# Attention and two mixtures of experts: maxima across partitions by TensorE, filler matmuls in blocks, two banks for batch 0's values, batch 1 held back

## The chip, the cores and the metric

The kernel runs on one core of a Trainium2 chip. Its time is the device time of one execution in microseconds, and of several executions the median counts. Five engines share the work: TensorE (PE in the profile; PEld are its weight loads), VectorE (DVE), ScalarE (ACT), GpSimd (POOL) and SyncE (SP, which here only issues DMAs). Each takes its instructions in the order in which they were written for it, and an instruction that waits holds up all behind it on its engine.

## The reference, cut to what matters

Three stages follow each other:

```python
# attention: 4 batches, 8 heads, 576 tokens, head size 64, float32
scores = q @ k.T / 8                       # heads 0-3: the last 32 keys; heads 4-7: every 32nd key
attn = softmax(where(mask, scores, -1e9))
x = (attn @ v)                             # written as 2304 tokens x 512
# first mixture: all 4 experts on all tokens
x = sum_e p[:, e:e+1] * (relu(x @ w1[e]) @ w2[e])      # 512 -> 1024 -> 512
# second mixture: 8 experts, each token goes to one (288 tokens each, by sorted gate logits)
out[mask_e] = relu(x[mask_e] @ v1[e]) @ v2[e]
```

Matrices of the mixtures are held as two float16 halves (a high part and what is left over), and a product takes three float16 matmuls. To make the halves, a tensor is first scaled by a power of two, which is found from its largest absolute value: a maximum along each partition, then one across the 128 partitions.

## The kernel before, in words

A small planner (class `Stream`) writes the program. Each task is a Python generator; it issues instructions, and yields how long it expects to wait. The planner keeps a clock of its own (`st.now`), advanced by the expected cost of every matmul, and `run`, `pick` and `till` keep a queue time for each other engine. So the order of instructions on every engine is fixed when the program is built, by the planner's costs. Nothing of the planner runs on the chip, where only the order and the data dependences count.

Attention works in units of two heads (`hp` 0 to 3: units 0 and 1 are local heads, 2 and 3 strided ones), in two halves each. A unit's q and k are turned by TensorE (`turn`, tiles `pk`, `pq`); for batch 0 this takes nine instructions for a turn, for later batches three. A half (`half_unit`) then computes scores (`pss`, 12 matmul instructions), masks and takes the row maximum on VectorE (L401), exponentiates on ScalarE (L407), multiplies by the reciprocal sums (L420; `pick` chooses VectorE or GpSimd), turns the probabilities (`turn_p`, tile `pp`), multiplies by the values (`po`), and splits the result into `xh` and `xl` (L452, L453). Batch 0's tiles of `po` use one PSUM bank.

While attention of batch 0 runs, weights of the first expert are loaded, their maximum is found (`measure`, `widest`), and they are split into `wh` and `wl` (`split`). The main loop starts layer 1 of expert 0 when batch 0's attention and this split are written. From then on TensorE does expert matmuls (`pl` of layer 1, `py` of layer 2), and the attention of batches 1 to 3 is written between them. Tokens of an expert go in five groups (512, 512, 256, 512, 512), and group 1 of expert 0 needs batch 1.

`widest` (L217) finds a maximum across partitions by GpSimd's `partition_all_reduce` (L224), and VectorE then computes the scale (L230 to L236). `load_gate` (L713) scales the gate's weights in this way. `keep_warm` (L466) is called when the planner has a gap, and writes matmuls that nobody reads; with the gaps that the planner sees, the program has none of them. A loop of the planner starts at L976.

## Time and profile before

| what | value |
|---|---|
| median of 3 runs | 1216.44 us (1211.65 to 1218.27) |
| profiled execution, its own time | 1209.59 us |
| its span, first to last instruction | 1207.9 us |
| PE busy | 1159.6 us, 96% |
| DVE busy | 767.3 us, 64% |
| ACT, POOL busy | 525.0 us (43%), 221.3 us (18%) |
| mean granted TensorE clock | 0.976 |

The span is cut by the profile into 40 slices, and busy shares are given for each. PEclk is the share of TensorE's full clock that was granted: 1.0 is 2.4 GHz, 0.5 is 1.2 GHz. Ends of matmuls are modelled and overlap, so the start of one to the start of the next is a better measure of what one costs than its duration. A bracket behind an instruction tells how long its engine was idle before it and whom it waited for; "issue" is idle time that no wait shown explains.

### The profile page before, as it was taken

The numbers are of one execution on the slowest core, as the hardware profiler recorded it, in microseconds if no ns is written. First come the engines' busy times: TensorE is split into PE (matmuls) and PEld (weight loads), VectorE is DVE, ScalarE is ACT, GpSimd is POOL, SyncE is SP. The second block draws the span as 40 slices with busy tenths as digits, with TensorE's granted clock in tenths as the row PEclk, the third lists the DMA queues.
The fourth block names the chain that finished last, engine by engine and source line by source line (L and its number), as shares of the span: only waits on it lengthen the run. The fifth ranks groups of instructions, "written<-read, shape, count | busy, mean of one in ns | idle before, by whom it ended". The sixth has DMA issues, their size and how long they took to land.

```text
span 1207.9 us, 20992 instructions
## 1 busy us (share of the span) xinstructions
PE 1159.6 (96%) x7989; PEld 684.8 (57%) x7989; DVE 767.3 (64%) x2186; ACT 525.0 (43%) x1151; POOL 221.3 (18%) x346
## 2 busy tenths in 40 slices
PE   8939999999999999999999999999989899999998
PEld 6726565664444464444464445654534477777887
DVE  3849986737675557675568877874367766666310
ACT  3637555523542424453444356645323333333444
POOL 3021300010101111111110001010034332334333
PEclk9858999999999999999999999999999999999999
DMA  9342454211338434444732242321003354555631
GB/s 234 76 118 61 100 186 83 77 50 62 113 105 278 140 140 139 140 139 167 252 122 88 71 139 84 126 97 62 1 36 112 119 176 164 180 180 179 248 111 41
DMA packets 87774, 150.84 MB, mean 125 GB/s; under 512 B 48313, under 2 KB 53689, under 8 KB 85626
## 3 DMA queue, kind: packets, MB, share of 16 engines
q1 hardware_dynamic: 74106, 104.09, 28.1%
q0 software_dynamic: 13568, 45.41, 10.5%
q8 instruction: 63, 1.03, 0.4%
q14 instruction: 37, 0.30, 0.1%
HBM read 106.44 MB, written 45.37 MB: 126 GB/s over the span
## 4 chain that ended last, share of the span: by engine, by line
PE 78%; DVE 6%; issue 2%; POOL 1%; DMA 1%; ACT 0%; POOLq 0%; ACTq 0%
PE py L123 35%; PE pl L123 34%; PE pss L123 1%; DVE ohr L1307 1%; PE po L123 1%; PE pp L127 1%; PE pc L123 1%; PE pyt L127 1%; PE pxt L127 1%; DMA out_dram<-ot,ix 1%; DVE ge L1150 1%; PE pi L123 1%; PE th L123 0%; PE pcs L123 0%; PE po L127 0%
## 5 line engine op out<-in xcount | busy, mean ns | idle before, releaser
L123 PE MATMUL py<-wh,h 128*128 128x512 f16 x1024 | 311.5, 379 | 0.9 <-DVE h L639 0.9
L123 PEld LDWEIGHTS <-h 128*128 128x128 f16 x1600 | 148.6, 98 | 168.0 <-DVE h L639 1.4
L123 PE MATMUL pl<-xh,wh 128*128 128x512 f16 (+1 forms) x640 | 229.5, 359 | 0.0
L123 PE MATMUL pl<-xl,wh 128*128 128x512 f16 (+1 forms) x640 | 229.3, 358 | 0.0
L123 PE MATMUL pl<-xh,wl 128*128 128x512 f16 (+1 forms) x640 | 229.3, 358 | 0.0
L123 PE MATMUL py<-wl,h 128*128 128x512 f16 x512 | 194.1, 379 | 0.0
L123 PEld LDWEIGHTS <-wh 128*128 128x128 f16 x1280 | 124.2, 98 | 117.3 <-issue 0.3
L635 ACT ACTIVATE t<-pl 128x512 f32<-128x512 f32 (+1 forms) x160 | 88.8, 555 | 213.7 <-PE pl L123 203.9
L639 DVE TENSOR_TENSOR h<-t,h 128x512 f16<-128x512 f32 (+1 forms) x144 | 91.4, 639 | 87.0 <-ACT h L636 87.0
L123 PE MATMUL pl<-xT,wa 128*128 128x288 f16 x768 | 108.3, 289 | 0.0
L123 PE MATMUL py<-hT,wb 128*128 128x288 f16 (+2 forms) x864 | 106.6, 273 | 0.2 <-POOL hT L1414 0.2
L925 ACT ACTIVATE po<-pr,v_s 128x1024 f16<-128x1024 f32 x64 | 73.1, 1150 | 70.2 <-DVE v_s L236 30.6
L123 PEld LDWEIGHTS <-wl 128*128 128x128 f16 x640 | 62.5, 98 | 58.4 <-issue 0.4
L927 DVE SCALAR_TENSOR_TENSOR po<-pr,v_s,po 128x1024 f16<-128x1024 f32 x64 | 82.0, 1282 | 18.4 <-ACT po L925 18.2
L123 PEld LDWEIGHTS <-wb 128*128 128x128 f16 x864 | 73.4, 98 | 14.5 <-issue 0.5
L123 PEld LDWEIGHTS <-wa 128*128 128x128 f16 x768 | 71.5, 99 | 17.4 <-issue 0.3
L636 ACT ACTIVATE h<-pl 128x512 f16<-128x512 f32 (+1 forms) x144 | 78.7, 547 | 0.0
L912 DVE TENSOR_REDUCE pam<-pr 128x1 f32<-128x1024 f32 x64 | 76.5, 1208 | 0.0
L407 ACT ACTIVATE sm<-sm,mx 96x128 f32<-96x128 f32 (+2 forms) x152 | 58.0, 388 | 19.4 <-DVE mx L401 19.4
L677 DVE SCALAR_TENSOR_TENSOR ysb<-py,pe,ysb 128x512 f32<-128x512 f32 x42 | 31.5, 749 | 46.2 <-PE py L123 45.9
L1414 POOL TENSOR_TENSOR hT<-t,hT 128x288 f16<-128x288 f32 x64 | 49.1, 780 | 35.4 <-ACT hT L1413 26.3
L1412 ACT ACTIVATE t<-pl 128x288 f32<-128x288 f32 x64 | 26.2, 409 | 61.9 <-PE pl L123 55.9
(293 smaller groups left out, 1572.0 us busy)
## 6 DMA issues: line engine op xcount, KB each, us to landing
pr<-in_moe_w_dram SPq DMA_DIRECT2D x64, 512.0 KB, 4.0
raw<-in_moe_w_dram SPq DMA_DIRECT2D x32, 512.0 KB, 7.6
w1d<-po POOLq DMA_DIRECT2D x32, 512.0 KB, 5.2
w2d<-po POOLq DMA_DIRECT2D x32, 512.0 KB, 5.1
wa<-w1d SPq DMA_DIRECT2D x8, 2048.0 KB, 8.2
wb<-w2d SPq DMA_DIRECT2D x8, 2048.0 KB
yd<-yr SPq DMA_DIRECT2D x18, 257.0 KB, 6.3
qn<-in_q_dram SPq DMA_DIRECT2D x24, 144.0 KB, 2.9
```

The source lines that it names most:

```text
L123: nc.tensor.matmul(o, a, b, start=first, stop=last)
L127: nc.tensor.transpose(o, a, i)
L407: nc.scalar.activation(sm[j][0:nq, t, 0:nk], sm[j][0:nq, t, 0:nk], AF.Exp, bias=mx[0:nq, 0, j, t:t + 1], scale=-1.0, accum_out=mx[0:nq, 1, ...
L635: nc.scalar.activation(t[:, 0:n], pl[:, 0:n], AF.Relu, scale=HS)
L636: nc.scalar.activation(hh[:, 0, 0:n], pl[:, 0:n], AF.Relu, scale=HS)
L639: nc.vector.tensor_sub(hh[:, 1, 0:n], t[:, 0:n], hh[:, 0, 0:n])
L677: nc.vector.scalar_tensor_tensor(ysb[:, j], py, pe, ysb[:, j], op0=ALU.mult, op1=ALU.add)
L912: nc.vector.tensor_reduce(am[:, c:c + 1], chunks[4 * m + c], AX.XY, ALU.max, apply_absolute_value=True)
L925: nc.scalar.activation(h, r, AF.Copy, scale=s_)
L927: nc.vector.scalar_tensor_tensor(l, r, s_, h, op0=ALU.mult, op1=ALU.subtract)
L1412: nc.scalar.activation(t, pl, AF.Relu, scale=HS)
L1414: nc.gpsimd.tensor_sub(hT[:, f, 1], t, hT[:, f, 0])
```

## The change

Six things change in the program's text.

1. `widest` no longer calls GpSimd. TensorE transposes the 128 per-partition maxima (spread over 128 columns) into a PSUM tile `pm`, and VectorE reduces it. All 30 uses take this path.
2. Fillers: `keep_warm` collects the planner's gaps, and when 0.9 us is owed it writes a block of matmuls (128x128 by 128x256, float16), one for each 0.15 us, all into one PSUM tile that lasts until batch 0 is done. 18 of them stand at the start.
3. Batch 0's `po` tiles use the two banks of `ps_m`, since the bank of `ps_o` holds the fillers' tile.
4. Units of batch 1 wait until six of batch 0's eight halves are written.
5. Costs change: scores, values and some turns are booked as cheaper on TensorE, the second multiplication of a half as dearer on VectorE, the exponentials as cheaper; the scaled copy `xh` goes to VectorE or ScalarE by `pick`.
6. `load_gate` becomes a task of its own, 30 us later in the planner's clock.

```diff
+        yield till(run("V", 0.2)) + 0.3
+        yield from take("tr")
+        pm = ps_t.tile([P, P], F32, name=f"{name}_pm{uid()}", tag="tr")
+        tr(pm, amax.to_broadcast([P, P]), ident, 0.107)
+        yield 0.3
         g = sp.tile([P, 1], F32, name=f"{name}_g", tag="p2g", bufs=2)
-        nc.gpsimd.partition_all_reduce(g, amax, channels=P, reduce_op=bass_isa.ReduceOp.max)
+        nc.vector.tensor_reduce(g, pm, AX.X, ALU.max)
+        run("V", 0.25)
+        give_back("tr")
...
-                mm(pss[j][0:nq, t, 0:nk], qT[rows, 32 + W * i:32 + W * i + nq], kT[rows, k0:k0 + nk], True, True, 0.213)
+                mm(pss[j][0:nq, t, 0:nk], qT[rows, 32 + W * i:32 + W * i + nq], kT[rows, k0:k0 + nk], True, True, 0.105)
...
-            eng, t = pick(ready_at, V=0.5, G=1.0)
+            eng, t = pick(ready_at, V=0.5 + 0.7 * j, G=1.1)
...
-        yield from take("po")
-        po = ps_o.tile([P, 3 * W], F32, name=f"po{nm}", tag="po")
+        pool, tag = (ps_o, "po") if b else (ps_m, "mm")
+        yield from take(tag)
+        po = pool.tile([P, 3 * W], F32, name=f"po{nm}", tag=tag)
...
+        eng, t = pick(V=0.55, A=0.6)
...
-        nc.vector.tensor_scalar(hi, src, xs[b], None, op0=ALU.mult)
+        if eng is nc.vector:
+            eng.tensor_scalar(hi, src, xs[b], None, op0=ALU.mult)
+        else:
+            eng.activation(hi, src, AF.Copy, scale=xs[b])
+            yield till(t)
...
     def keep_warm(gap):
-        n = int(gap / 0.107)
-        if n > 2:
-            pw = ps_m.tile([P, 2 * P], F32, name=f"warm{uid()}", tag="mm")
-            for _ in range(n - 1):
-                mm(pw, ident16, ident.bitcast(F16), True, True, 0.0)
+
+        owed[0] += gap
+        if owed[0] > 0.9:
+            warm_up(int(owed[0] / 0.15))
+            owed[0] = 0.0
+
+    def warm_up(n):
+        if not warmth:
+            warmth.append(ps_o.tile([P, 2 * P], F32, name="warm", tag="po"))
+        for _ in range(n):
+            mm(warmth[0], ident16, ident.bitcast(F16), True, True, 0.0)
...
+            while b == 1 and worth.get(0, 0) < 2 * NHP - 2:
+                yield 0.2
...
-                load_gate()
-                run("V", 2.0)
+                st.add(load_gate(), 30.0)
...
     st.fill = keep_warm
+    spare["po"] = 0
+    warm_up(18)
+    st.spend(6.0)
     st.until(lambda: att_done[0] >= 1 and (0, 0) in ready_w)
     st.fill = None
+    give_back("po")
```

How this moves instructions is seen at three places. On GpSimd, from the clearing of the first two `kT` tiles on, this stood before (`vs` is the permuted copy of the strided heads' values, `x_g`, `w_g`, `wg_g` are maxima across partitions, "ISA" alone sets up GpSimd's code):

```order
L482 MEMSET kT_0_171 128x32
L482 MEMSET kT_1_206 128x32
L224 ISA
L224 ISA x_g<-x_a_250 128x1
L249 DMA vs<-in_v_dram 18x32x64 x8
L224 ISA w_g<-w_a_493 128x1
L482 MEMSET kT_0_529 128x32
L253 MEMSET vl_654 32x4x64
L620 ISA
L620 TENSOR_SCALAR raw_0_163<-raw_0_163,w_s 128x1024
L621 TENSOR_TENSOR wl_0_612<-raw_0_163,wh_0_611 128x1024
L224 ISA
```

And this stands there now:

```order
L509 MEMSET kT_0_190 128x32
L509 MEMSET kT_1_231 128x32
L259 DMA vs<-in_v_dram 18x32x64 x4
L430 TENSOR_TENSOR xl<-xl,mx_0_1_304 96x384
L259 DMA vs<-in_v_dram 18x32x64 x4
L430 TENSOR_TENSOR xl<-xl,mx_1_1_448 96x384
L430 TENSOR_TENSOR sm_2_0_1_544<-sm_2_0_1_544,mx_2_0_522 126x3x126
```

The all-reduces, the split of a weight chunk and the set-ups of code between them are gone from this stretch. The second multiplication of a half is on GpSimd, and the copy of batch 0's values no longer stands behind an instruction that needs the maximum. In the whole program 38 such multiplications are on GpSimd, where none was.

On TensorE, this stood before the first matmul of layer 1 (`pl0_0_0`; the digit behind a name's letters is the batch):

```order
L127 MATMUL pq1_2_1_924<-ident_69,qn1_2_788 128x96 x3
L127 MATMUL pp1_0_0_1_930<-ident_69,sm1_0_0_1_752 128x96 x3
L123 MATMUL pss1_1_1_0_941<-kT1_1_715,qT1_1_714 96x128 x3
L123 MATMUL pss1_1_1_1_945<-kT1_1_715,qT1_1_714 96x128 x3
L127 MATMUL pp1_0_1_0_959<-ident_69,sm1_0_1_0_819 128x96 x3
L127 MATMUL pp1_0_1_1_971<-ident_69,sm1_0_1_1_823 128x96 x3
L123 LDWEIGHTS wh0_0_611
L123 MATMUL pl0_0_0_990<-xh_113,wh0_0_611 128x512
```

And shortly before it there stands now:

```order
L123 MATMUL warm_170<-ident_69,ident16_74 128x256
L123 MATMUL pss1_0_1_0_989<-kT1_0_848,qT1_0_847 96x128 x3
L123 MATMUL pss1_0_1_1_993<-kT1_0_848,qT1_0_847 96x128 x3
L123 LDWEIGHTS ident16_74
L123 MATMUL warm_170<-ident_69,ident16_74 128x256
```

Before, three units of batch 1 were turned by then, four of its halves scored and two turned back. Now one unit is turned and its two halves are scored; 198 fillers stand ahead of the first `pl`, in blocks of 6 to 18.

On VectorE, the gate's weights stood before in this way, between the split of the first weights and the results of batch 0's unit 2:

```order
L716 TENSOR_REDUCE amg<-wgr 128x1
L230 TENSOR_SCALAR wg_g_703<-wg_g 128x1
L232 TENSOR_SCALAR wg_e<-wg_g_703 128x1
L234 TENSOR_SCALAR wg_i<-wg_e 128x1
L236 RECIPROCAL wg_s<-wg_i 128x1
L719 TENSOR_SCALAR wgc<-wgr,wg_s 128x4x8
L720 SCALAR_TENSOR_TENSOR wgc<-wgr,wg_s,wgc 128x4x8
L452 TENSOR_SCALAR xh<-po_2_0_721,x_s 128x18x21
L453 SCALAR_TENSOR_TENSOR xl<-po_2_0_721,x_s,xh 128x18x21
```

At the same place stands now:

```order
L636 SCALAR_TENSOR_TENSOR wl_0_805<-raw_0_163,w_s,wh_0_804 128x1024
L378 COPY sm_3_0_1_677<-pp_3_0_1_841 126x3x126
L636 SCALAR_TENSOR_TENSOR wl_0_805<-raw_0_163,w_s,wh_0_804 128x1024 x3
L469 SCALAR_TENSOR_TENSOR xl<-po_3_0_887,x_s,xh 128x18x21
L411 ISA sm_0_0_0_954,mx_0_0_937<-pss_0_0_0_938,ml_77 96x128
```

The gate's scale no longer stands there; it is now behind the start of layer 1, between the results of expert 0's first group. All four chunks of `wl` are on VectorE.

## Rows read from the trace of the kernel before

**Rows 1.** From the page: slices of the span, busy tenths and granted clock.

```profile
PE   8939999999999999999999999999989899999998
...
PEclk9858999999999999999999999999999999999999
```

**Rows 2.** Stages: length, busy us (instructions) of each engine, granted clock, DMA share, GB/s.

```profile
347.00:860.00 513.00, 513.00 (x2972) 257.07 (x2970) 344.47 (x637) 232.65 (x356) 50.69 (x93) 1.00 0.38 130
97.00:347.00 250.00, 249.09 (x1624) 139.32 (x1623) 182.37 (x586) 120.10 (x376) 27.71 (x56) 0.99 0.34 97
0.00:97.00 97.00, 71.92 (x460) 57.02 (x461) 58.21 (x244) 46.68 (x168) 16.83 (x35) 0.78 0.57 139
```

**Rows 3.** The same by tens of us: PE, PEld, DVE, ACT, POOL, clock.

```profile
30.00:40.00 10.00, 10.00 (x62) 8.00 (x61) 6.44 (x25) 5.60 (x22) 0.00 (x0) 1.00 0.47 120
40.00:50.00 10.00, 8.17 (x74) 6.43 (x74) 8.67 (x35) 5.97 (x26) 0.48 (x2) 0.85 0.01 2
50.00:60.00 10.00, 9.90 (x83) 8.32 (x81) 9.48 (x46) 7.69 (x21) 0.30 (x1) 0.64 0.44 97
60.00:70.00 10.00, 1.68 (x19) 1.28 (x16) 2.50 (x4) 4.16 (x21) 4.75 (x2) 0.70 1.03 308
70.00:80.00 10.00, 0.24 (x3) 0.27 (x5) 2.64 (x13) 0.15 (x1) 0.67 (x3) 0.50 0.38 58
80.00:90.00 10.00, 8.96 (x56) 7.12 (x55) 9.68 (x46) 6.36 (x30) 0.81 (x3) 0.50 0.00 1
```

**Rows 4.** Timeline of 57 to 80 us: start, us, engine, line, instruction [idle before].

```profile
65.17 2.85 POOL L620 TENSOR_SCALAR raw<-raw,w_s 128x1024 f32<-128x1024 f32 x1 [7.77 <-issue]
...
76.74 0.38 POOL L224 PARTITION_ALL_REDUCE wg_g<-amg  x1 [6.51 <-issue]
77.15 0.15 DVE L230 TENSOR_SCALAR wg_g<-wg_g 128x1 f32<-128x1 f32 x1 [14.65 <-POOL wg_g L224]
79.76 0.93 PE L123 MATMUL po<-sm,vt 126*64 126x126 f32 x8 [16.91 <-DVE xl L453]
```

**Rows 5.** Timeline, PE: attention's instructions at either clock, and the first layer matmuls.

```profile
32.64 2.13 PE L123 MATMUL pss<-kT,qT 64*96 64x128 f32 x12
59.53 1.19 PE L123 MATMUL pss<-kT,qT 64*96 64x128 f32 x12
97.02 0.63 PE L123 MATMUL pl<-xh,wh 128*128 128x512 f16 x1
102.22 0.66 PE L127 MATMUL pp<-ident,sm 96*128 96x96 f32 x6
103.80 0.41 PE L127 MATMUL pk<-ident,kn 96*128 96x96 f32 x3
```

**Rows 6.** Chain of waits, longest pieces of 260 to 450 us: start, us, what.

```profile
263.96 20.72 PE pl L123 x96
...
429.72 10.48 PE pl L123 x96
```

**Rows 7.** Timeline, DVE and POOL: batch 0's scores, values, maxima, and a pair at 124 us.

```profile
13.06 0.28 DVE L401 CUSTOM_DVE_ANT_0 xh<-pss,ml 96x128 f32<-96x128 f32 x1
17.17 6.85 POOL L249 DMA_DIRECT2D vs<-in_v_dram  x8
82.29 1.81 DVE L274 TENSOR_REDUCE vam<-vl 128x1 f32<-128x768 f32 x2
94.19 1.02 DVE L420 TENSOR_TENSOR sm<-sm,mx 96x384 f32<-96x384 f32 x2
124.21 2.13 POOL L621 TENSOR_TENSOR wl<-raw,wh 128x1024 f16<-128x1024 f32 x1
124.77 2.12 DVE L639 TENSOR_TENSOR h<-t,h 128x512 f16<-128x512 f32 x1
```

**Rows 8.** From the page and the groups by line: xcount, busy us, mean ns.

```profile
L639 DVE TENSOR_TENSOR h<-t,h 128x512 f16<-128x512 f32 (+1 forms) x144 | 91.4, 639 | 87.0 <-ACT h L636 87.0
L865 POOL TENSOR_TENSOR ysb<-yt,ysb 128x512 f32<-128x512 f32 x11 | 15.0, 1367 | 13.0 <-ACT yt L864 12.9
```

More of the change, by code (lines that the diff above doesn't have):

```diff
@@ L136, in tile_attn_moe_moe @@
     queue = {}
+    busy = {}
     def run(engine, cost, after=0.0):
+        busy[engine] = busy.get(engine, 0.0) + cost
         queue[engine] = max(queue.get(engine, 0.0), st.now, after) + cost
@@ L239, in pow2 @@
     def pow2(amax, n, name, pool=None):
-        return pow2_of(widest(amax, n, name), name, pool)
+        g = yield from widest(amax, n, name)
+        return pow2_of(g, name, pool)
     xs = {}
@@ L278, in x_wide @@
     def x_wide(b):
-        XG[b] = widest(XM[b], 4, "x")
+        XG[b] = yield from widest(XM[b], 4, "x")
     def x_scale(b):
@@ L326, in turn @@
                     if j:
-                        mm(pq[j * D:(j + 1) * D, c, :], a, ident[0:96, 0:96], True, True, 0.16)
+                        mm(pq[j * D:(j + 1) * D, c, :], a, ident[0:96, 0:96], True, True, 0.12)
                     else:
-                        tr(pq[j * D:(j + 1) * D, c, :], a, ident[0:96, 0:96], 0.107)
+                        tr(pq[j * D:(j + 1) * D, c, :], a, ident[0:96, 0:96], 0.125)
             if is_local(hp):
@@ L408, in half_unit @@
                                      scale=-1.0, accum_out=mx[0:nq, 1, j, t:t + 1])
-        yield till(run("A", 1.18 * len(tiles))) + 0.1
+        yield till(run("A", 0.1 + 0.78 * len(tiles))) + 0.1
         for t0, t1, nq, nk in parts:
@@ L437, in half_unit @@
                 vv = vs_[b][0][:, h, i, :] if local else vs_[b][0][0:nk, i, h - NHL, :]
-                mm(po[j * D:(j + 1) * D, t * W:t * W + nq], vv, sm[j][0:nk, t, 0:nq], True, True, 0.14)
+                mm(po[j * D:(j + 1) * D, t * W:t * W + nq], vv, sm[j][0:nk, t, 0:nq], True, True, 0.065)
         if not own:
@@ L451, in half_unit @@
             src = po[:, 0:nr * 18].rearrange("d (r a) -> d a r", a=18)
-        nc.vector.tensor_scalar(hi, src, xs[b], None, op0=ALU.mult)
+        if eng is nc.vector:
[3 more added lines that the diff above has]
+            yield till(t)
         nc.vector.scalar_tensor_tensor(lo, src, xs[b], hi, op0=ALU.mult, op1=ALU.subtract)
-        yield till(run("V", 1.1))
-        give_back("po")
+        yield till(run("V", 0.55, t))
+        give_back(tag)
         worth[b] = worth.get(b, 0) + 1
@@ L461, in tile_attn_moe_moe @@
     att_done = [0]
+    owed = [0.0]
+    warmth = []
     def keep_warm(gap):
-        n = int(gap / 0.107)
-        if n > 2:
-            pw = ps_m.tile([P, 2 * P], F32, name=f"warm{uid()}", tag="mm")
-            for _ in range(n - 1):
-                mm(pw, ident16, ident.bitcast(F16), True, True, 0.0)
+        owed[0] += gap
[7 more added lines that the diff above has]
+            mm(warmth[0], ident16, ident.bitcast(F16), True, True, 0.0)
     def attention():
@@ L532, in scale_x @@
         run("V", 1.6)
-        x_wide(b)
-        yield till(run("G", 0.5, run("V", 0.2))) + 0.5
+        yield from x_wide(b)
         x_scale(b)
@@ L545, in first_scale @@
         run("V", 1.3)
-        x_wide(0)
-        yield till(run("G", 0.5, run("V", 0.2))) + 0.5
+        yield from x_wide(0)
         x_scale(0)
@@ L572, in max_w @@
         nc.vector.tensor_reduce(wam[x][:, c:c + 1], chunk(raws[x], x, c), AX.X, ALU.max, apply_absolute_value=True)
-        if c == 3:
-            wwide[x] = widest(wam[x], 4, f"w{x}")
-    def find_w(x):
-        wsc[x] = pow2_of(wwide[x], f"w{x}")
     def room_w(e, x):
@@ L588, in measure @@
                 yield till(run("V", 1.25)) + pause
-            yield till(run("G", 0.5)) + 0.5
-            find_w(x)
+            wsc[x] = yield from pow2(wam[x], 4, f"w{x}")
             yield till(run("V", 0.8)) + 0.1
@@ L615, in split @@
             r, h, l = [chunk(t, x, c) for t in [raws[x]] + wts[x]]
-            eng, t = pick(V=1.2) if e else pick(V=1.2, G=4.0)
+            eng, t = pick(V=1.2) if e else pick(V=1.2, G=5.0)
             if eng is nc.vector:
@@ L716, in load_gate @@
         nc.vector.tensor_reduce(am, raw, AX.XY, ALU.max, apply_absolute_value=True)
-        s_, inv = pow2(am, 1, "wg")
+        run("V", 0.2)
+        s_, inv = yield from pow2(am, 1, "wg")
+        run("V", 1.5)
         gc = cp.tile([P, KD, 2, E2], F16, name="wgc")
@@ L810, in gate_of_last @@
         nc.vector.tensor_reduce(am, Gs, AX.XY, ALU.max, apply_absolute_value=True)
-        g = widest(am, 1, "G")
-        yield till(run("G", 0.5, run("V", 0.25))) + 0.5
+        run("V", 0.2)
+        g = yield from widest(am, 1, "G")
         s_, inv = pow2_of(g, "G", lp)
@@ L913, in prepare @@
                 yield till(run("V", 1.25)) + 1.0
-            g = widest(am, 4, f"v{x}")
-            yield till(run("G", 0.5, run("V", 0.2))) + 0.5
+            g = yield from widest(am, 4, f"v{x}")
             s_, inv = pow2_of(g, f"v{x}")
@@ L937, in tile_attn_moe_moe @@
     raw_at, vn_at = {}, []
-    raws, wam, wwide, wsc, wts, ready_w = {}, {}, {}, {}, {}, set()
+    raws, wam, wsc, wts, ready_w = {}, {}, {}, {}, set()
     warm = sp.tile([P, 1], F32, name="warm")
```

## The prediction

> **What bounds the kernel now.** I read the page first: in its 40 slices TensorE is busy nine tenths or more nearly everywhere from the fifth slice on, and only the first ones show a hole and a granted clock below full [rows 1]. The table by stages says the same in numbers. From 97 to 347 us (the stage of expert 0, into which batches 1 to 3 are woven) TensorE is busy 249.1 of 250 us, from 347 to 860 us all of it; in the first 97 us only 71.9, at a mean clock of 0.78 [rows 2]. So a microsecond of TensorE work saved or added behind 97 us is a microsecond of the kernel, and the first 97 us are a stage by itself, which ends when batch 0 and the first weights are ready. I call that end T0; before, it is 97.0, where the first `pl` stands [rows 5].
>
> Inside that stage two things are seen. First a hole: from 60 to 80 us TensorE has 1.9 us of work [rows 3]. The timeline names the cause: GpSimd spends 7.8 us on "issue" ahead of a weight split, whose first half takes 2.85 us, 6.5 us more on "issue" behind it, and only then does the all-reduce of the gate's maximum; VectorE waits 14.65 us for it, and TensorE 16.9 us for VectorE [rows 4]. Nothing of batch 0 needs the gate's scale. Second, the clock. A block of 12 score instructions takes 2.13 us at 32 us and 1.19 us at 59 us [rows 5], so the first 40 us ran at the lower level (1.2 GHz), although the column of the clock shows 1.00 there. From 40 us TensorE has gaps at the higher level (8.2 of 10 us busy, clock 0.85 over that stretch), the next ten are at 0.64, and after the hole it is at 0.5 [rows 3].
>
> **The change part by part.** I count against the profiled execution: 1209.6 us, of which the span is 1207.9 and 1.7 lie around it. The median is 6.8 us above it, and I add that at the end.
>
> T0 first. What goes: the hole's 14.65 us, since the gate's maximum now stands behind the start of layer 1 and GpSimd has no all-reduce and no split ahead of it. That alone gives 82.4. Work leaves VectorE as well, which was busy 9.5 to 9.7 of 10 us on both sides of the hole [rows 3] and so set the pace there: of its 58.2 us up to T0 [rows 2], the scoring of batch 1's later halves, the maxima of batch 1's values, two halves' sums and multiplications, one multiplication in each of six halves of batch 0, and seven scaled copies go elsewhere, while one chunk of `wl` (1.3 us) comes; by the timeline's durations (0.28 us a scored tile, 0.51 us a multiplication or copy, 1.81 us for half of the maxima [rows 7]) I estimate 16 us less (13 tiles 3.6, 17 multiplications and copies 8.7, maxima 3.4, small ones 1.6, less the chunk), of which 12 were in the crowded parts. 82.4 less 12 gives T0 = 70.
>
> That has to be held against TensorE. Busy up to T0 was 71.9 us, mostly at half clock; turned into full clock stretch by stretch (half up to 40 us, from 47 to 57 and from 64 on) it is about 41 us, of which 11 were batch 1's. What remains, with 4 us of batch 1's first unit, is 34 us. To it come 198 fillers. A 256-column float16 matmul costs 10.48 us / 96 = 0.109 us at full clock [rows 6], together 21.6. So with the start at 2.3 us, T0 can't be below 58 if the clock is full all along; at half clock throughout it would be 2.3 + 2 x 55.6 = 113.5. These are the two ends. I take 70 because VectorE's count ends there, and because it leaves TensorE 12 us for gaps and for stretches at half clock. The first 18 fillers are among these: at half clock they take 3.9 us, ahead of batch 0's first turn. Term: 97 - 70 = -27, bounds -39 to +16.5.
>
> Batch 1 held back: before T0 stood three units' turns (12 groups at 0.41), four halves' scores (at 1.19) and two halves' `pp` (at 0.66) [rows 5], together 11.0 us at full clock; now one unit's turns and two halves' scores, 4.0. The difference, 7.0 us, moves behind T0, where TensorE has no room. Term: +7 (these durations include each block's tail, so 5 to 7).
>
> Maxima by TensorE: 30 transposes, 28 of them behind T0. Their like is `pp`, 0.66 / 6 = 0.11 us [rows 5]: +3. The new thing is that TensorE waits in order for a VectorE reduction; queued behind it are expert matmuls. The planner books 0.3 us behind that reduction before it writes the transpose, and by its costs TensorE lost 0.9 us in all in the 250 of expert 0's stage [rows 2], so I take no wait; if each cost 0.5 us, it would be 14 more.
>
> First layer matmuls: at T0 the clock was low, a `pl` of 512 columns took 0.63 us [rows 5]; the stage's mean clock of 0.99 [rows 2] makes this some 5 us at half clock, worth 2.5. With fillers up to T0 it should be full: -2 (0 to -2.5).
>
> The second multiplication on GpSimd: 30 of them (38 instructions), 24 behind T0. No row shows this one; GpSimd's float32 `ysb` addition takes 1.367 us for 512 columns [rows 8], so about 1.03 for 384. It runs beside VectorE's multiplication of the same half. One place shows what such a pair can do: while GpSimd's `wl` ran for 2.13 us, an `h` on VectorE that takes 0.64 us in the mean took 2.12, and ended about half a microsecond behind GpSimd's [rows 7, 8]. So VectorE may lose up to 1.03 us for each, 24.7 us in all at the worst. Behind T0 VectorE is busy 182 of 250 us [rows 2] and loses some 20 us of work to GpSimd and ScalarE, which covers the loss, save where a turned half comes late to TensorE. Term: +3 (0 to 25).
>
> The Trainium skill states a rule here, in "SBUF — State Buffer", section "Who interferes with whom": an instruction of VectorE with two SBUF inputs contends with a GpSimd instruction that reads SBUF, and the loser blocks for the whole instruction. The row on `h` agrees with it. By the rule the two multiplications of a half run one behind the other, which is the third rival below; without it the term would be 0.
>
> What costs nothing: the copy of `vs` for batch 0 no longer waits for the maximum (it was issued at 17.2 us behind it [rows 7], and can now go at some 4 us, beside the first loads); its values are needed only by unit 2, some 40 us later. The copies `xh` on ScalarE are covered by ScalarE's 120 of 250 us. Experts 1 to 3, the routing and the second mixture have the same instructions.
>
> Sum: -27 + 7 + 3 - 2 + 3 = -16. The profiled execution would be 1193.6, the median **1200**.
>
> **The rivals.** (1) The clock stays at the lower level in spite of the fillers. For it: TensorE was wholly busy from 20 to 40 us and ran at half clock all the same. Against: while it is at half clock the fillers leave no gaps, and later stretches of dense work were at full clock throughout [rows 1]. Then 198 fillers cost 43 us and T0 is 113.5: +16.5 + 7 + 3 + 3 = +29.5, 1246; nothing is gained from T0 = 85 on, and from 91 on the kernel is slower by half a per cent. (2) The clock comes and goes, or the first weights come late, and T0 is 80 to 92. For it: 8.2 us busy in 10 were followed by a fall [rows 3], and 55.6 us of work in 70 is no denser. At 86: -11 + 7 + 3 - 1 + 3 = +1, 1217. (3) GpSimd's multiplications hold up VectorE, and halves come late to TensorE, which has no fillers behind T0. At T0 = 74 and 20 us of such waits: -23 + 7 + 3 - 2 + 20 = +5, 1221. Against it: VectorE's spare time. (4) The hole goes, and every cover holds: T0 = 58, -39 + 7 + 3 - 2 = -31, 1185.
>
> **How the numbers follow.** The forecast (T0 from 62 to 80, 1191 to 1210 in the median) gets 0.66, the fourth case 0.08, the second 0.12, the third 0.07, the first 0.07. The range from 1185 to 1222 leaves out the first and the edges. Half a per cent, 6 us, is what a measurement of this kernel can tell from no change: faster 0.74 (forecast and fourth), same 0.12 (the second), slower 0.14 (first and third).
>
> **What would show it.** Right: no wait of VectorE for GpSimd in the first 80 us; the first `pl` at 62 to 80 us; TensorE's clock above 0.8 in the mean up to there; expert 0's stage 6 to 12 us longer than 250 (7 + 3 + 3 - 2 = 11); from its end to the last instruction as before within 4 us. Wrong: T0 above 85, a mean clock near 0.5 ahead of it, `h` or multiplications on VectorE of over 1 us in number, idle time of TensorE ahead of a `pp` or a `pm`, or a `pl` of group 1 that waits for batch 1.

## The result, and the profile after

The changed kernel takes 1186.70 us in the median of four runs (1184.15 to 1188.11), the kernel before 1217.36 in the four runs beside it: a ratio of 0.9752, 95% interval 0.9712 to 0.9793. That is faster, as was forecast, and inside the range of 1185 to 1222, but 13 us below the 1200: the time lies under the forecast's own 1191 to 1210 and beside the 1185 of the fourth rival, while the first `pl` (below) stands inside the forecast's 62 to 80 us. The profiled execution took 1184.15 us, of which 1182.1 are the span, against 1209.6 and 1207.9.

The slices of TensorE's busy share and of its clock, which answer to [rows 1]:

```profile
PE   9999999999999999999999999999999899999998
...
PEclk9999999999999999999999999999999899999999
```

The hole in the third slice is gone, and the clock column has no slice below 9. (Its first slice showed 9 before as well, when the clock was at the lower level there; the duration of a block of scores, below, tells the two apart.) The stages, which answer to [rows 2] (columns: stretch, its length, busy us and instructions of PE, PEld, DVE, ACT and POOL, clock, DMA share, GB/s):

```profile
0.00:63.93 63.93, 61.84 (x600) 50.00 (x601) 42.86 (x181) 41.52 (x144) 17.64 (x41) 1.00 0.74 182
63.93:317.50 253.57, 253.02 (x1691) 143.70 (x1689) 178.79 (x587) 135.62 (x434) 47.34 (x75) 1.00 0.37 102
317.50:860.00 542.50, 540.14 (x3176) 272.09 (x3175) 365.05 (x708) 240.28 (x370) 46.89 (x87) 1.00 0.36 124
```

The cuts are the first `pl` (T0, 63.93 us; before 97.02) and the first `pl` of expert 1 (317.50; before 346.68). So T0 came 33.1 us earlier, expert 0's stage is 3.9 us longer (253.57 after, 249.66 before), and the rest of the span is 3.4 us longer (864.6 after, 861.2 before): -25.8 us. The first stage by tens of us, which answers to [rows 3]:

```profile
30.00:40.00 10.00, 10.00 (x117) 8.38 (x118) 7.44 (x31) 7.81 (x29) 2.04 (x3) 1.00 1.06 302
40.00:50.00 10.00, 10.00 (x105) 8.33 (x106) 8.15 (x47) 7.74 (x36) 1.94 (x3) 1.00 0.16 57
50.00:60.00 10.00, 10.00 (x99) 8.41 (x97) 9.20 (x18) 7.76 (x21) 4.05 (x12) 1.00 0.15 35
60.00:70.00 10.00, 10.00 (x76) 6.32 (x75) 9.24 (x37) 7.01 (x30) 2.72 (x2) 1.00 0.85 164
```

From its first filler at 2.04 us to T0 TensorE has no gap, while VectorE is below 9.3 of 10 everywhere: the engine that sets T0 is now TensorE, with its fillers. The timeline of the same kernel shows what it does there (start, us, engine, line, instruction):

```profile
2.04 3.81 PE L123 MATMUL warm<-ident,ident 128*128 128x256 f16 x18 [2.04 <-DVE ident L183]
5.69 0.41 PE L127 MATMUL pk<-ident,ysb 96*64 96x96 f32 x3
...
10.58 1.17 PE L123 MATMUL pss<-kT,qT 64*96 64x128 f32 x12
...
41.66 0.55 DVE L430 TENSOR_TENSOR sm<-sm,mx 126x378 f32<-126x378 f32 x1
41.76 1.12 POOL L430 TENSOR_TENSOR sm<-sm,mx 126x378 f32<-126x378 f32 x1 [4.31 <-DVE mx L423]
...
47.09 0.32 PE L127 MATMUL w_pm<-ident,w_a 128*128 128x128 f32 x1
47.91 0.28 DVE L231 TENSOR_REDUCE w_g<-w_pm 128x1 f32<-128x128 f32 x1
```

The very first scores, at 10.6 us, take 1.17 us a block, as at full clock before, where the same block still took 2.13 at 32 us [rows 5]. The two multiplications of a half start 0.1 us apart on VectorE and GpSimd and end after 0.55 and 1.12 us. A maximum across partitions is now a transpose and a reduction of 0.28 us, and no GpSimd row stands between them.

### The profile page after: what moved, and what is told of

Same layout as the page of the kernel before. It is cut to its first block, busy times and chain, and to the rows that moved or that the text cites. A ratio compares the mean times of both kernels' runs of the same rounds, so it can differ in the third digit from the quotient of the medians.

```text
span 1182.1 us, 21448 instructions
## 1 busy us (share of the span) xinstructions
PE 1156.0 (98%) x8217; PEld 685.0 (58%) x8217; DVE 751.8 (64%) x2144; ACT 534.9 (45%) x1186; POOL 229.5 (19%) x352
## 3 DMA queue, kind: packets, MB, share of 16 engines
q0 software_dynamic: 13568, 45.41, 10.6%
## 4 chain that ended last, share of the span: by engine, by line
PE 89%; DVE 7%; issue 2%; POOL 1%; DMA 1%; ACT 0%; POOLq 0%; DVEq 0%; ACTq 0%
PE pl L123 36%; PE py L123 36%; PE pss L123 3%; PE warm L123 2%; PE po L123 2%; PE pp L127 1%; DVE ohr L1330 1%; PE pc L123 1%; PE pk L127 1%; PE pq L127 1%; PE pyt L127 1%; PE pxt L127 1%; PE po L127 1%; DVE ge L1173 1%; PE pi L123 1%
## 5 line engine op out<-in xcount | busy, mean ns | idle before, releaser
L123 PEld LDWEIGHTS <-wl 128*128 128x128 f16 x640 | 62.5, 98 | 57.8
L123 PEld LDWEIGHTS <-wa 128*128 128x128 f16 x768 | 71.4, 99 | 18.8 <-issue 2.1
L932 DVE TENSOR_REDUCE pam<-pr 128x1 f32<-128x1024 f32 x64 | 76.6, 1210 | 0.0
L948 POOL DMA_DIRECT2D w2d<-po x32 | 21.6, 674 | 248.9 <-DVE po L946 230.3
L948 POOL DMA_DIRECT2D w1d<-po x32 | 21.7, 678 | 230.5 <-DVE po L946 215.6
L417 ACT ACTIVATE sm<-sm,mx 96x128 f32<-96x128 f32 (+2 forms) x152 | 57.9, 387 | 1.3 <-DVE mx L411 1.3
```

The lines of the kernel that those rows point to most:

```text
L123: nc.tensor.matmul(o, a, b, start=first, stop=last)
L417: nc.scalar.activation(sm[j][0:nq, t, 0:nk], sm[j][0:nq, t, 0:nk], AF.Exp, bias=mx[0:nq, 0, j, t:t + 1], scale=-1.0, accum_out=mx[0:nq, 1, ...
L932: nc.vector.tensor_reduce(am[:, c:c + 1], chunks[4 * m + c], AX.XY, ALU.max, apply_absolute_value=True)
L948: nc.gpsimd.dma_start(dst[e, :, :, c * sz:(c + 1) * sz, :].rearrange("p l a b -> p l (a b)"), o.rearrange("p l a b -> p l (a b)"))
```

## The experiments

All starts in this table are those of `pl` instructions in each run's profiled execution. The start of expert 1 sums what the change moves (first stage and expert 0's stage), and in the two pairs of runs of one program it repeats within 0.8 us; the last part of the kernel is left out of it, since it differs between executions of one and the same program (below). Three parts of the change have no run of their own: the two banks for batch 0's values (in every run but "before" and "before + maxima"), the changed costs, and the gate's scaling as a task of its own.

| kernel | first pl (T0) | expert 0's stage | expert 1 starts | time over before, 95% interval |
|---|---|---|---|---|
| before | 97.0 | 249.7 | 346.7 | 1 |
| before + maxima by TensorE | 88.4 | 255.5 | 343.9 | 0.9975 (0.9956 to 0.9994) |
| before + fillers | 88.8 | 251.4 | 340.2 | 0.9941 (0.9911 to 0.9971) |
| before + both | 71.4 | 253.5 | 324.8 | 0.9832 (0.9796 to 0.9867) |
| the change | 63.9 | 253.6 | 317.5 | 0.9752 (0.9712 to 0.9793) |
| the change again | 63.6 | 253.6 | 317.2 | 0.9763 (0.9734 to 0.9791) |
| - no fillers | 70.5 | 254.4 | 324.9 | 0.9856 (0.9823 to 0.9888) |
| - only the first 18 fillers | 56.5 | 255.6 | 312.2 | 0.9800 (0.9760 to 0.9840) |
| - half of the later fillers | 57.1 | 253.6 | 310.7 | 0.9727 (0.9703 to 0.9752) |
| - the same again | 57.9 | 253.6 | 311.5 | 0.9712 (0.9687 to 0.9738) |
| - batch 1 not held back | 69.9 | 250.4 | 320.3 | 0.9778 (0.9753 to 0.9802) |
| - multiplications on VectorE | 62.6 | 260.8 | 323.3 | 0.9827 (0.9798 to 0.9857) |
| - all-reduce on GpSimd | 72.9 | 277.8 | 350.7 | 1.0049 (1.0027 to 1.0072) |
| - all-reduce, and mult. on VectorE | 61.7 | 265.7 | 327.4 | 0.9829 (0.9791 to 0.9867) |

### Fillers left out

Theory A gave the better part of the gain to the clock, which the fillers hold; theory B to the hole and to VectorE's lighter load.

```diff
     def warm_up(n):
...
-        for _ in range(n):
-            mm(warmth[0], ident16, ident.bitcast(F16), True, True, 0.0)
+        return
```

> The changed kernel (first pl at 63.9 us, span 1182.1) without any of its 198 fillers; the rest stands in the same order. Theory A (the higher clock, which the fillers hold, gives the better part of the gain before the first pl): TensorE runs at 1.2 GHz for most of the first stage again, its 35 to 40 us of work take up to twice that, first pl at 74 to 88 us, span 1193 to 1209. Theory B (the gain is the hole that went and the work that left VectorE; VectorE sets the pace and the clock is of no account): first pl at 58 to 64 us, span 1176 to 1183, since 24.6 us of fillers go from a TensorE that had no gap.

```diff
-        for _ in range(n):
+        for _ in range(n if st.now == 0 else 0):        # the first 18 alone
```

> The changed kernel with only its first 18 fillers (2.0 to 5.9 us); the 180 later ones are left out. Theory A: the clock rises at 5.5 us as before, then falls back in the gaps, and the first pl stands at 68 to 82 us, span 1186 to 1201. Theory B: as without fillers, first pl at 58 to 64, span 1176 to 1183. A third theory, A': the first block alone is enough, since the attention's own matmuls hold the clock once it is up: mean clock above 0.95, first pl at 50 to 60, span 1168 to 1179.

```diff
-        for _ in range(n):
+        for _ in range((n + 1) // 2 if n < 18 or st.now > 0 else n):
```

> The changed kernel with its first 18 fillers and about half of each later block. Theory A with TensorE as the bound (fillers are on the path at 0.124 us each): if the clock holds, the first pl comes some 8 to 11 us earlier, 53 to 56 us, span 1171 to 1174; if it falls, 66 to 78 us, span 1184 to 1196. Theory B (VectorE sets the pace, fillers only fill): first pl at 62 to 64 us, span 1180 to 1183.

The three programs keep the change's order of all other instructions. Without fillers T0 is 70.5 and the span 1188.8: neither 74 to 88 and 1193 to 1209 (A) nor 58 to 64 and 1176 to 1183 (B). The gain of the fillers as a whole is 7.4 us at the start of expert 1. Its stretches from 30 us on (columns as above; the clock column stands ahead of the DMA share) and two blocks of scores:

```profile
30.00:40.00 10.00, 10.00 (x61) 8.00 (x61) 6.62 (x31) 5.54 (x18) 4.36 (x5) 1.00 1.01 292
40.00:50.00 10.00, 9.03 (x93) 7.15 (x91) 7.54 (x32) 8.36 (x36) 1.71 (x2) 1.00 0.13 39
50.00:60.00 10.00, 6.97 (x58) 5.12 (x58) 8.49 (x49) 8.58 (x34) 3.02 (x6) 0.83 0.00 0
60.00:70.00 10.00, 8.57 (x56) 7.17 (x57) 9.12 (x22) 6.37 (x19) 2.38 (x11) 0.59 0.46 96
```

The two blocks, from the timeline of the same run:

```profile
32.91 2.13 PE L123 MATMUL pss<-kT,qT 64*96 64x128 f32 x12
...
41.63 1.25 PE L123 MATMUL pss<-kT,qT 64*126 64x126 f32 x12
```

Here too TensorE is wholly busy from 30 to 40 us and does only 61 instructions, where the change does 117: the block of 2.13 us says half clock, though the column says 1.00. It is at the higher level from about 41 us; behind 50 us, with 6.97 of 10 us busy, the clock falls (0.83 in the mean), and from 62 us to T0 it is at the lower level (0.59 over the last row).

With the first 18 alone T0 is 56.5, 14 us earlier than with none, and earlier than the change's own; expert 1 starts 12.7 us earlier than with none. In time this isn't shown: the medians are 1188.5 and 1194.8 us and their intervals overlap, since the last part was long in this version (below), so that it isn't faster than the change (1186.7) either. Its stretches:

```profile
40.00:50.00 10.00, 6.56 (x58) 4.57 (x56) 9.69 (x34) 9.40 (x31) 4.06 (x12) 0.85 0.13 47
50.00:60.00 10.00, 10.00 (x51) 6.82 (x50) 8.98 (x34) 6.92 (x32) 0.95 (x1) 0.50 0.89 187
60.00:70.00 10.00, 10.00 (x70) 5.91 (x69) 5.91 (x17) 5.62 (x13) 1.32 (x3) 0.97 0.10 25
```

From 6 us into the ten behind 40 it ran at full clock on attention's work alone; then TensorE had gaps, and the clock fell to 0.50 up to T0 and into the first layer matmuls, which made expert 0's stage 2.0 us longer than the change's. So A' holds for the first 40 us only (T0 is in its range, the mean clock up to T0, 0.92, and the span, 1183.6, are not), and the later fillers do hold the clock; but all 180 are too many. Half of them keep it at 1.00, and T0 is 57.1:

```profile
40.00:50.00 10.00, 9.11 (x92) 6.89 (x91) 9.34 (x47) 9.19 (x31) 4.11 (x9) 1.00 0.13 46
50.00:60.00 10.00, 9.50 (x82) 6.75 (x82) 9.97 (x35) 8.00 (x35) 0.77 (x6) 1.00 0.67 144
```

TensorE has gaps again and VectorE reaches 9.97 of 10. That T0 moved so far falsifies B for the changed kernel. That it moved 6.8 us, and not to 53 to 56, suggests that VectorE is close behind: the 90 fillers were worth 10.4 us, at the 0.116 us from start to start of the change's later ones (the 0.124 of the expectation has the first 18 in it, which were mostly at the lower clock). That VectorE is what bounds this version is read from the row, not tested.

### One part alone, and both

```diff
-        nc.gpsimd.partition_all_reduce(g, amax, channels=P, reduce_op=bass_isa.ReduceOp.max)
...
+        tr(pm, amax.to_broadcast([P, P]), ident, 0.107)
...
+        nc.vector.tensor_reduce(g, pm, AX.X, ALU.max)   # on before: widest as a generator, nothing else
```

> The kernel before (first pl at 97.0 us, span 1207.9) with the maxima across partitions by TensorE and VectorE in place of GpSimd's all-reduce, and nothing else of the change. Theory B: the hole of 14.65 us goes whole, first pl at 80 to 84 us, span 1194 to 1199 (with 3 us for 30 transposes). Theory A: without a higher clock TensorE, which has 72 us of work at mostly 1.2 GHz up to the first pl, soon becomes the bound, and GpSimd's split still comes late: first pl at 86 to 94 us, span 1200 to 1208.

```diff
+            warmth.append(ps_o.tile([P, 2 * P], F32, name="warm", tag="po"))   # on before: keep_warm and warm_up
...
+    spare["po"] = 0                                                           # of the change, batch 0's po
+    warm_up(18)                                                               # in ps_m, nothing else
```

> The kernel before with the fillers of the change alone (the first block of 18, the later blocks of 0.15 us booked each, 192 in all, their lasting tile, and batch 0's po in the other pool for that); the all-reduce on GpSimd, batch 1's early start and all else as before. Theory A (the clock gives the better part): full clock from 5.5 us on, the stretch up to the gate's maximum shrinks by about 10 us, the hole (VectorE 14.65 us for GpSimd) stays, behind it no half clock: first pl at 74 to 84 us (97.0 before), span 1183 to 1194. Theory B (hole and VectorE's work give it): first pl at 90 to 97 us, span 1201 to 1208, since the maxima by TensorE alone brought it from 97.0 to 88.4 already.

Each alone moved T0 by some 8 us and the kernel by 0.25% and 0.6%. The maxima alone have T0 where A had it (the span, 1209.4, is 1.4 above); the fillers alone come nearest to B, T0 1.2 below its range and the span 0.6 above. With the maxima alone the hole is gone, but the clock is not up (two stretches of that run):

```profile
70.00:80.00 10.00, 7.68 (x51) 5.97 (x47) 9.75 (x37) 5.13 (x26) 9.80 (x14) 0.52 1.07 284
80.00:90.00 10.00, 8.21 (x53) 6.30 (x51) 9.43 (x49) 6.42 (x24) 0.00 (x0) 0.50 0.29 68
```

VectorE is the busier engine in these two (9.75 and 9.43 of 10), and TensorE has gaps: that TensorE is the bound there, as A had it, is not shown by them. With the fillers alone all goes faster up to the gate's maximum, and then waits for it (timeline of that run):

```profile
63.05 2.12 POOL L631 TENSOR_TENSOR wl<-raw,wh 128x1024 f16<-128x1024 f32 x1
71.07 0.38 POOL L224 PARTITION_ALL_REDUCE wg_g<-amg  x1 [5.90 <-issue]
71.48 0.15 DVE L230 TENSOR_SCALAR wg_g<-wg_g 128x1 f32<-128x1 f32 x1 [18.52 <-POOL wg_g L224]
```

Its stretch from 60 to 70 us:

```profile
60.00:70.00 10.00, 0.00 (x0) 0.00 (x0) 0.00 (x0) 0.00 (x0) 5.08 (x3) 0.50 0.52 78
```

VectorE began to wait at 53.0 us (71.48 less 18.52); before it did so at 62.5 [rows 4]. The clock brought 9.5 us, of which the hole, grown from 14.65 to 18.52 us, took 3.9; in it the clock fell again: fillers that are written behind the waiting scores wait with them. So the two parts should be worth more together than their sum:

```diff
+    # on before: both of the edits above, and nothing else
```

> The kernel before with the fillers of the change and the maxima by TensorE, and nothing else: the gate's maximum stays where it stood, batch 1 isn't held back, all multiplications stay on VectorE. Alone, the maxima moved the first pl from 97.0 to 88.4 us and the fillers to 88.8. Theory D (each part takes away one of two things that hold the first stage up, and one left is enough to hold it): with both, more than the sum of the two goes: first pl at 66 to 74 us, expert 0's stage 250 to 256, span 1181 to 1191. Theory S (the parts add up, and the rest of the gain is the hold-back and the multiplications): first pl at 78 to 82 us, span 1191 to 1200.

T0 is 71.4 and expert 1 starts 21.9 us earlier than before, against 2.8 + 6.5 = 9.3 for the two apart: theory D. The span alone, 1192.7, would fit S and lies 1.7 above what D allowed; from expert 1 on it took 867.8 us, the change 864.6, a difference of the size that one program shows from run to run (below).

### The all-reduce put back

```diff
-        tr(pm, amax.to_broadcast([P, P]), ident, 0.107)
...
-        nc.vector.tensor_reduce(g, pm, AX.X, ALU.max)
...
+        nc.gpsimd.partition_all_reduce(g, amax, channels=P, reduce_op=bass_isa.ReduceOp.max)
```

> The changed kernel with GpSimd's all-reduce for the maxima across partitions in place of the transposes and reductions; fillers, hold-back and the rest as in the change. Theory A: the clock stays full, and the all-reduces that stand among GpSimd's splits and multiplications cost little, since the planner has other work to put beside them: first pl at 62 to 67 us, expert 0's stage 250 to 255 us, span 1179 to 1187. Theory B: the hole comes back at 6 to 8 us for each change between the two kinds of GpSimd work, VectorE waits for GpSimd by over 8 us in the first 80: first pl at 70 to 80 us, span 1188 to 1199.

B has T0 (72.9), and behind T0 both theories were too mild: expert 0's stage is 24 us longer than the change's, the span is 1215.5, and the kernel is half a per cent slower than before. (The planner writes 192 fillers here and not 198, as in the next run.) The timeline of its worst place, GpSimd and the TensorE instruction that waits for it:

```profile
101.01 2.53 POOL L633 TENSOR_TENSOR wl<-raw,wh 128x1024 f16<-128x1024 f32 x1
...
109.49 0.38 POOL L226 PARTITION_ALL_REDUCE wg_g<-amg  x1 [5.95 <-issue]
...
116.81 1.60 POOL L424 TENSOR_TENSOR sm<-sm,mx 96x384 f32<-96x384 f32 x2 [6.94 <-issue]
117.68 0.74 PE L127 MATMUL pp<-ident,sm 96*128 96x96 f32 x3 [15.40 <-POOL sm L424]
```

Each time that GpSimd goes from arithmetic to the all-reduce or back, 5.8 us or more pass ahead of the instruction; in the two rows here the profile names no wait for them. In the kernel before this stood on the path once, for the gate; with multiplications of attention on GpSimd it stands between VectorE and TensorE again and again (TensorE waits 27.7 us for `sm` in four places). The Trainium skill, "GPSIMD Engine Reference", section "Instruction dispatch", says that the first call to a freshly loaded kernel costs about 6 us with no visible instruction; the rows of 5.95 and 6.94 agree in size, and they come again at each change, not the first alone, though nothing in them shows that code is loaded. The test is to take the going back and forth away, with the all-reduce still there:

```diff
+        nc.gpsimd.partition_all_reduce(g, amax, channels=P, reduce_op=bass_isa.ReduceOp.max)   # as above
-            eng, t = pick(ready_at, V=0.5 + 0.7 * j, G=1.1)
+            eng, t = pick(ready_at, V=0.5)
```

> The changed kernel with the all-reduce on GpSimd (which alone cost over 30 us of span) and with the second multiplication on VectorE, so that GpSimd no longer goes back and forth between all-reduces and multiplications. Theory K (each change of kind on GpSimd costs 6 to 7 us of idle time ahead of the instruction, and the multiplications multiplied those on the path): the waits of TensorE for GpSimd's sm go, first pl at 62 to 70 us, expert 0's stage 250 to 260, span 1183 to 1198. Theory R (the all-reduces themselves hold the kernel up wherever they stand): first pl at 70 to 76, stage 268 to 280, span 1205 to 1217.

The waits of TensorE for GpSimd's `sm` are gone, expert 1 starts at 327.4 and not at 350.7. T0 is 0.3 us below K's range, the span (1194.0) in it, expert 0's stage 5.7 us above it (TensorE waits once 6.8 us for `h`). R is out: the all-reduces by themselves, with the multiplications on VectorE in both kernels, cost 4.1 us (327.4 against 323.3); with the multiplications on GpSimd they cost 33.2 (350.7 against 317.5), so 29 of these come only where the two kinds of work are mixed.

This run shows one thing more. T0 is 61.7 us with every maximum on GpSimd: with the multiplications on VectorE, the hole of the first stage is gone as soon as the gate's all-reduce stands behind T0. Timeline of this run:

```profile
100.38 0.38 POOL L226 PARTITION_ALL_REDUCE wg_g<-amg  x1 [5.86 <-issue]
```

In time, too, the kernel with the multiplications on VectorE is the same with the maxima on either engine (0.9829 and 0.9827). So what the transposes buy here is mainly that GpSimd is free for multiplications; that the gate's place takes the hole away by itself was not tested apart from the rest of the change.

### Holding batch 1 back, and the multiplications

```diff
-            while b == 1 and worth.get(0, 0) < 2 * NHP - 2:
-                yield 0.2
```

> The changed kernel without the wait that holds batch 1 back (216 fillers in place of 198, six more turned groups and one more half of scores up to the first pl). If TensorE with its fillers is the bound up to the first pl (as the trace of the change reads): 18 more fillers at 0.124 us are 2.2 us, the batch 1 work 3 to 5 us; first pl at 68 to 71 us, expert 0's stage 3 to 5 us shorter (249 to 251), span 1183 to 1187. If VectorE's chain were the bound, its work for batch 1 would come on top: first pl at 70 to 76, stage 248 to 251, span 1185 to 1191.

T0 at 69.9, stage 250.4, span 1187.9. The first sentence has T0 and the stage and misses the span by 0.9, the second has stage and span and misses T0 by 0.1: the run doesn't tell the two apart. (Up to T0 its trace has 24 more scores, which is two halves and not the one expected.) What it does show: what is not held back costs more ahead of T0 (5.9 us, of which 2.0 are 18 more fillers) than it saves behind it (3.1 us). The 2.8 us between are read from one trace each; in time the two kernels are not told apart (0.9778 against 0.9752 and 0.9763, with intervals that overlap).

```diff
-            eng, t = pick(ready_at, V=0.5 + 0.7 * j, G=1.1)
+            eng, t = pick(ready_at, V=0.5)
```

> The changed kernel with the second multiplication of each half on VectorE (0.55 us each, 38 of them) in place of GpSimd. If the two engines' instructions held each other up, as in the rival of the prediction, nothing is lost and the kernel is the same or faster: first pl 62 to 64, span 1175 to 1182. If they run beside each other and TensorE is the bound up to the first pl, VectorE's 8 more multiplications up to there (4.4 us) fit partly: first pl at 64 to 67, stage 253 to 256, span 1182 to 1188.

Expert 1 starts 5.8 us later and the kernel is slower than the change: the multiplications do help on GpSimd. Of the first branch T0 fits (62.6) and the span does not (1189.9 against 1175 to 1182); the second was too low with both the stage and the span, and 1.4 us too high with T0. T0 came 1.3 us earlier, as 24 fewer scores are written ahead of it; the stage is 7.2 us longer, by those 24 scores and by gaps of TensorE (1.4 us ahead of a `po` for VectorE's `xl`, 1.0 for a turned `qT`, 0.7 for `sm`).

### The change and the version with half the fillers, side by side

The first kernel has no edit, the second is that with half of each later block.

> The changed kernel once more, beside the version with half of the later fillers. By the traces: first pl at 63.9 us within 0.3, span 1180 to 1184.

> The changed kernel with half of each later block of fillers, once more, beside the changed kernel on the same chip. If the 6.8 us by which the first pl came earlier are a gain of the kernel: first pl at 57.1 us within 0.3, the median 5 to 7 us below the changed kernel's. If the last part of the kernel (from expert 3's start on, 485.8 us here against 483.5) gives part of it back each time: 3 to 5 us below.

Medians 1186.95 (1182.85 to 1188.49, six runs) and 1180.34 (1178.68 to 1181.28, six): 6.6 us apart, without overlap. This version beats both kernels; nothing was given back. Its T0, 57.9, is 0.5 above what I had allowed. The change's span here, 1185.1, is 1.1 above what I had allowed, with T0 as before. Where it comes from, the last part shows, from expert 3's last matmul to the end (columns as above). Before:

```profile
947.12:1207.80 260.68, 245.79 (x2423) 194.20 (x2421) 126.93 (x520) 99.68 (x212) 95.26 (x123) 0.99 0.46 160
```

The change:

```profile
919.48:1182.10 262.62, 245.98 (x2423) 194.03 (x2421) 124.73 (x520) 99.35 (x212) 94.17 (x123) 0.98 0.46 159
```

The change again:

```profile
919.18:1185.00 265.82, 249.03 (x2423) 195.89 (x2421) 124.30 (x520) 99.61 (x212) 93.76 (x123) 0.97 0.45 157
```

The change with the first 18 fillers alone:

```profile
915.77:1183.50 267.73, 250.47 (x2423) 195.82 (x2421) 125.73 (x520) 99.66 (x212) 94.85 (x123) 0.96 0.45 156
```

The instructions are the same 2423, the clock goes from 0.99 to 0.96, and the length from 260.7 to 267.7 with it. Two executions of one program differ by 3.2 us, so none of this part's difference is put down to the change. Where these two part can be seen: both have a gap of TensorE of 1.4 us shortly before 1072 us, and behind it the clock stays up in the one and falls in the other. The change, and the change again:

```profile
1073.00:1080.00 7.00, 7.00 (x77) 5.34 (x76) 3.04 (x13) 3.08 (x8) 4.94 (x6) 1.00 0.45 139
```

```profile
1073.00:1080.00 7.00, 7.00 (x50) 4.89 (x49) 1.92 (x10) 1.61 (x4) 4.28 (x5) 0.51 0.48 159
```

Seven us at half the clock are half that in lost work, 3.5 us, which is about the difference. The run with the first 18 alone has such stretches at 1040 to 1045 us (0.66) and 1075 to 1080 us (0.72).

## Why the prediction was right, and where it was off

It was right in kind: the hole went, the clock was up, T0 fell inside the 62 to 80 of the forecast, and what was added behind T0 was small against it. It was too cautious in size: nearly every term erred to the slow side, and the time came out under the forecast's 1191 to 1210, close to the 1185 that had a chance of 0.08 only; of its signs of being right, the 6 to 12 us by which expert 0's stage was to grow failed (3.9). That T0 fell inside 62 to 80 is in part luck, since another engine set it than the one I counted. By its terms:

- **T0, -27 forecast, -33.1 measured.** The step "I take 70 because VectorE's count ends there" failed. It left out what the higher clock does ahead of the hole: there TensorE set the pace (VectorE 6.44 of 10 us busy from 30 to 40 us, [rows 3]), and the fillers alone brought VectorE to the gate's maximum 9.5 us sooner. By an estimate, 70 less 9.5 is 60.5, below TensorE's own floor, so the floor decided; the versions with fewer fillers, which start at 56.5 to 57.9, agree. The 16 us of work that I saw leave VectorE were right (58.2 before [rows 2], 42.9 now).
- **The floor, 58 forecast, 63.9 measured**, with no gap in it: 2.0 to the start, 24.6 of fillers (3.7 for the first 18, mostly at the lower clock, and 0.116 us from start to start for each of the other 180; I took 0.109 for all 198 in the floor), 37.3 of attention and maxima (I took 34). Of the 12 us that 70 was to leave TensorE, only 6 were there.
- **Batch 1, +7 forecast, +5.4 measured** by the matmuls that are more behind T0: 24 scores at 0.090, 12 `pp` at 0.097 and 24 turns at 0.085 us from start to start. My price was block durations, which hold a tail, and the lower end of 5 to 7 was the better one. That it is bought back, by 5.9 us ahead of T0 against 3.1 behind it, is read from the trace of the run without the hold-back.
- **Transposes, +3, as forecast:** 28 behind T0, 0.11 us each, no gap ahead of any. Only 9 stand in expert 0's stage (1.0 us) and 19 behind it, so my 11 us for that stage counted 2 too many, and for the rest I should have said 2 more.
- **First layer matmuls, -2 forecast, -2.3 to -2.5 found.** Before, the first 4.6 us of the stage ran at the lower clock (0.50 from 97 to 101 us, 0.69 in the next), which is worth 2.3; taken by starts, the matmuls that both stages have are 2.5 shorter. Attention's matmuls have their part in it, not the first layer's alone.
- **GpSimd's multiplications, +3 forecast, none found on TensorE's path.** The groups by line of the change show a VectorE multiplication of 0.553 us in the median beside GpSimd's of 1.088 (duration in ns: least, median, most):

```profile
L430 DVE TENSOR_TENSOR sm<-sm,mx x36: 265/553/555, 41.7 to 221.8; 96x384 f32<-96x384 f32 x12, 126x378 f32<-126x378 f32 x8, 126x126 f32<-126x126 f32 x8, 72x72 f32<-72x72 f32 x8
L430 POOL TENSOR_TENSOR sm<-sm,mx x36: 297/1088/1706, 41.8 to 222.1; 96x384 f32<-96x384 f32 x12, 126x378 f32<-126x378 f32 x8, 126x126 f32<-126x126 f32 x8, 72x72 f32<-72x72 f32 x8
```

A piece of that size takes VectorE as long alone. Only the smallest pieces got longer, by 0.2 us; the groups by line and shape (count | busy us, mean ns) from 100 to 310 us, before:

```profile
L420 DVE TENSOR_TENSOR sm<-sm,mx 126x378 f32<-126x378 f32 x12 | 6.1, 549 | 0.2
...
L420 DVE TENSOR_TENSOR sm<-sm,mx 72x72 f32<-72x72 f32 x12 | 2.7, 223 | 0.0
```

and of the change:

```profile
L430 DVE TENSOR_TENSOR sm<-sm,mx 126x378 f32<-126x378 f32 x6 | 3.3, 554 | 0.2
L430 DVE TENSOR_TENSOR sm<-sm,mx 72x72 f32<-72x72 f32 x6 | 2.5, 423 | 0.0
```

Eight such pieces make 1.6 us of VectorE's time, beside work, and TensorE had no gap for it. The third rival had VectorE blocked for GpSimd's whole instruction. In the pairs with large pieces VectorE starts 0.1 us ahead and loses nothing; it is GpSimd that is held up. In the run with the all-reduce put back, two of its 96x384 pieces with no VectorE instruction beside them took 1.60 us together, 0.8 each (the row at 116.81 us above); beside VectorE's multiplication such a piece takes 1.11 us in the median, and 1.71 where a second VectorE instruction with two inputs follows (timeline of the change):

```profile
68.25 0.55 DVE L430 TENSOR_TENSOR sm<-sm,mx 96x384 f32<-96x384 f32 x1
68.38 1.71 POOL L430 TENSOR_TENSOR sm<-sm,mx 96x384 f32<-96x384 f32 x1 [0.91 <-DVE mx L423]
68.72 0.68 DVE L657 TENSOR_TENSOR h<-t,h 128x512 f16<-128x512 f32 x1
```

The Trainium skill's rule ("SBUF — State Buffer", section "Who interferes with whom") is that an instruction of VectorE with two SBUF inputs contends with a GpSimd instruction that reads SBUF, and that the order of issue decides which of the two blocks. These rows agree with it, and so does the `h` of the prediction, which started behind GpSimd's `wl` [rows 7]: what the prediction had wrong is which engine would be the later one. In size the rows show less than a full block: 0.3 us more, where 0.4 us of VectorE's multiplication were still to run. GpSimd's lost time cost nothing here, as TensorE didn't wait for it. My upper price of 25 us came from the one `h` of 2.12 us [rows 7], in which GpSimd was first, and so was no measure of a multiplication in which VectorE is.

The stage then adds up: 5.4 + 1.0 - 2.5 = 3.9, as it must, since starts of matmuls leave nothing of TensorE's time out; the clock's 2.3 is the part that was found in another way. The sum was 9.8 us short of the 25.8 measured: 6 on T0, 3 on the multiplications, 1.6 on batch 1, 0.5 on the first layer, less 1.4 in the rest that is not the transposes. Some 4 us more of the 13 come from the step to the median: I added 6.8 us to the profiled execution, and the median stands 2.6 above it.

Of the rivals, the clock that stays low or comes and goes was real in the versions without enough fillers, not in the change. The prediction also took the parts one by one, and that they need each other it did not say: without the maxima on TensorE the rest of the change is no gain at all (1.0049), and becomes one (0.9829) when the multiplications go back to VectorE. It gave the hole's 14.65 us to two causes together, the gate's later place and the all-reduces that went; the run with the all-reduces on GpSimd and the multiplications on VectorE has T0 at 61.7 us with the first and without the second.

## What to carry to other kernels

Where two things hold a stage up in turn, here a hole and a low clock, each edit alone can look worthless; before dropping one, try it with the other, and price a stall by what would be late without it. Fillers are work: count them against the busiest engine of the stage, and take only as many as the clock asks for; the first block, ahead of all work, brought the first expert matmul 14 us forward here, and leaving out half of the later ones gained 6.6 us. And keep an engine that is slow to change its kind of work, as GpSimd between all-reduce and arithmetic, to one kind where others wait for it.

## What was not expected of the hardware

- A block of 18 fillers (3.8 us) ahead of the first real matmul had TensorE at 2.4 GHz from about 6 us on and, with no other filler, till behind 40 us. Without it the same instructions, with TensorE 10.00 of 10 us busy from 20 to 40 us, ran at 1.2 GHz up to about 41 us.
- A change of GpSimd between arithmetic and all-reduce cost 5.9 to 7.8 us in the rows above and in [rows 4].
- A GpSimd multiplication of 96x384 took 0.8 us alone, 1.11 in the median beside one of VectorE that had started 0.1 us before it, and 1.71 where a second one of VectorE followed.
- The granted clock of the last part went from 0.96 to 0.99 between executions, and with it its length: behind the same gap of 1.4 us the clock fell to 0.51 in one execution of the change and stayed at 1.00 in another. What decides this stays open, and so does the reason why it was lowest in the run with the first 18 fillers alone.
